# One matmul per sequence line for u: spectrum and low-rank rows stacked as 96 weight rows

## The chip, the cores and the metric

The kernel runs on one core of one Trainium2 chip. The metric is the device time of one execution in microseconds; the time before is the median of three runs. Engine names are those of the profile: PE is the matrix engine, PEld its weight loads, DVE, ACT and POOL the vector, scalar and general engines, SP the engine that here only issues DMAs.

## The reference

`x` has the shape (8, 3136, 256): eight batches, 3136 places in a sequence, 256 channels.

```
X = rfft(x, axis=1); Y = X * (filt_r + 1j * filt_i); y = irfft(Y, n=3136, axis=1)
h = y^T @ U @ V            # U is 3136 x 32, V is 32 x 3136
u = y + h^T
out = u + relu(u @ w_ch1) @ w_ch2      # 256 -> 1024 -> 256
```

All large products are done in float16 with float32 sums.

## The kernel before

The sequence is cut as 3136 = 64 x 49: a place is 49 q + r, with q from 0 to 63 and a "line" r from 0 to 48. A batch goes through these steps.

- **f1** (`f1_units`, L432): a 64-point transform over q for each line; the result goes through ACT or DVE into `asb` and by DMA to the DRAM tensor `c1`.
- **a** (`load_a`, L451): `c1` is read back in the other order, eight frequencies to a tile, 98 rows (49 lines, real and imaginary).
- **middle** (`stream`): per step m, `px` = forward transform over the lines (L466), the products with the filter on DVE (L485, L487; their sum on POOL, L490), `pi` = inverse transform over the lines (L502), evacuated by ACT into `esb` (L506). A step's `pi` is made two steps behind its `px` (LAG = 2). After four steps SP writes `esb` to the DRAM tensor `c2` (L508).
- **e** (`load_e`, L458): `c2` is read back into `e2`, 64 spectrum rows per line. Two lines stand one above the other, so that a tile of 128 rows holds 24 pairs of lines and the last line; one batch is one tile, and there are two such tiles. Four pairs of DMAs of 200 and 192 KB fill one.
- **h1** (`h1_unit`, L533): h1 = U^T y, from `e2` and the transformed U (`usb`), 25 matmuls into four column quarters of one PSUM tile that L537 (ACT) scales into the 128-row tile `h1` (four partial sums, not folded).
- **u** (`u_part`, in `make_u` and `make_odd`): for four pairs of lines and one half dh of the channels, one matmul of 512 columns adds the low-rank part (weights `h1`, moving `vr`, which holds V four times on top of itself, L555), and four of 128 columns add y itself (weights `e2`, moving the inverse 64-point transform `s2`, L560). ACT evacuates (L591, L594). The last line of each batch goes in `make_odd`, with 64 columns.
- **the channel network**: `mm1` (L601, evacuated with relu by L609 on ACT or L607 on DVE) and `mm2` (L627 or, "turned", L656, followed by L660 and L661 on DVE). SP and POOL send the results out (L669); from batch 2 on each group sends four DMAs on SP.

The order of the work on every engine is written out by hand. The outer loop runs over "groups" of four pairs of lines, six to a batch, of which the eight matmul pairs of `mm1` set the beat: a group has eight slots, a batch 48 (SB). `put(slot, gen)` hangs a piece of another stage into a slot, `run(slot)` issues it; an even slot runs behind the four L601 matmuls of two `mm1`, an odd one behind a quarter of `mm2` of the group before. `make_u` of the next group is issued in the third quarter, so that the first u of batch b stands about four slots ahead of slot 48 b. Within a slot, pieces are issued in the order in which they were put: the middle step first, then loads, then h1. Batch 0 has its own opening (`first_f1`, `first_a`, `first_mid`), ahead of slot 0. PSUM has four tags: `m` (four banks), `o` (two), `x` (one, for `px`) and `f` (one, which `pi` and `ph` of h1 share).

```
    steps = [9 + 1.5 * k for k in range(NP)] + [33 + 2.87 * k for k in range(NP)]
    for b in range(3, nb):
        steps += [SB * (b - 2) + 31 + 3 * k for k in range(NP)]
    ...
            put(t + (4 if b else 3), one(load_e, b + 1, m // GP))
    ...
        put(SB * b - 4, h1_unit(b))
```

V is brought into its layout in the opening: 14 POOL copies (L266), then seven matmuls with the selection matrix `sel` (L277, 32 weight rows) and seven ACT copies (L278) into `vr`, one of each in the opening and six in slots 1 to 11.

Of the kernel before, what the change touches and what calls it, by code (L numbers as in the profile page):

```python
# [21 lines left out]
KG = 8  # L22
# [4 lines left out]
def _consts():  # L27
# [21 lines left out]
    for s in range(NS):  # L49
        for j in range(49):  # L50
# [29 lines left out]
    return (w64.astype(f16), s2.astype(f16), np.eye(128).astype(f16),  # L80
            np.tile(np.eye(32), (1, 4)).astype(f16),
            np.ascontiguousarray(t2.transpose(1, 0, 2).reshape(98, NS * 128)).astype(f16),
# [5 lines left out]
def kernel(  # L88
# [12 lines left out]
    nb = x.shape[0]  # L101
    w64_np, s2_np, idn_np, sel_np, t2_np, g_np = _consts()
    w64_d = nc.inline_tensor(w64_np, name="w64d")
    s2_d = nc.inline_tensor(s2_np, name="s2d")
    idn_d = nc.inline_tensor(idn_np, name="idnd")
    sel_d = nc.inline_tensor(sel_np, name="seld")
    t2_d = nc.inline_tensor(t2_np, name="t2d")
# [35 lines left out]
    def load_x(b, c, parts=None):  # L143
        if c not in st[b].setdefault("x", {}):
            st[b]["x"][c] = sb.tile([128, 9 * DM], F16, tag="xt", bufs=6, name="xt")
        t = st[b]["x"][c]
        for lo, hi in parts or ((c0[c], c0[c + 1]),):
            for h in range(2):
                m = (hi - lo) // 4
                nc.gpsimd.dma_start(  # L150
                    t[64 * h:64 * h + 64, (lo - c0[c]) * DM:(lo - c0[c] + 4 * m) * DM]
                    .rearrange("p (m e) -> p m e", m=m),
                    bass.AP(tensor=x.tensor, offset=x.offset + (b * SEQ + 2 * lo + 4 * h) * DM,
                            ap=[[RD, NQ], [8 * DM, m], [1, 4 * DM]]))
            if hi == NH:
                o = (NH - 1 - c0[c]) * DM
                if b:
                    nc.gpsimd.memset(t[64:128, o:o + DM], 0.0)
                nc.gpsimd.dma_start(t[0:64, o:o + DM], rows(x, b, NR - 1, 1))
# [60 lines left out]
    for c in range(1, len(CH)):  # L220
        load_x(0, c)
    sel = cst.tile([32, 128], F16)
    nc.sync.dma_start(sel, sel_d.ap())
    s2 = cst.tile([128, 128], F16)
# [11 lines left out]
    load_x(1, 2)  # L236
    uq = sb.tile([64, NR * RANK], F16, tag="esb", bufs=2, name="uq")
    nc.gpsimd.dma_start(uq, moe_U.rearrange("(q r) p -> q (r p)", q=NQ))
    vqs = []
    for k in range(2):  # L240
        v = sb.tile([32, SEQ // 2], F16, tag="xt", bufs=6, name="vq")
        vqs.append(v)
        nc.gpsimd.dma_start(v, moe_V[:, k * (SEQ // 2):(k + 1) * (SEQ // 2)])
    w1 = cst.tile([128, 2 * 1024], F16)
# [7 lines left out]
    nc.gpsimd.dma_start(w2n, moe_w_ch2.rearrange("(t cc) e -> cc t e", t=8))  # L252
    vr = cst.tile([128, NH * 128], F16)
    usb = cst.tile([128, NH * RANK], F16)
    nc.vector.memset(usb[64:128, (NH - 1) * RANK:NH * RANK], 0.0)

    vps = []

    def v_order():

        for r0 in range(0, NH, 4):
            n, nh = (4, 2) if r0 < NH - 1 else (1, 1)
            vp = sb.tile([32, 512], F16, tag="h", bufs=18, name="vp")
            dst = vp[:, 0:n * nh * 64].rearrange("p (r h q) -> p r h q", h=nh, q=64)
            for k, v in enumerate(vqs):
                nc.gpsimd.tensor_copy(  # L266
                    dst[:, :, :, 32 * k:32 * k + 32],
                    bass.AP(tensor=v.tensor, offset=v.offset + 2 * r0,
                            ap=[v.ap[0], [1, n], [4, nh], [NR, 32]]))
            vps.append((r0, n * nh * 64, vp))  # L270
            yield

    def v_units():

        for r0, n, vp in vps:
            pv = bank("m", "pv")
            nc.tensor.matmul(pv[:, 0:n], sel[:, :], vp[:, 0:n], start=True, stop=True)  # L277
            nc.scalar.copy(vr[:, r0 * 128:r0 * 128 + n], pv[:, 0:n])  # L278
            yield

    def new_e2(b):
        e2 = sb.tile([128, NH * DM], F16, tag="e2", bufs=2, name="e2")
        (nc.gpsimd if b else nc.vector).memset(e2[64:128, (NH - 1) * DM:NH * DM], 0.0)
        st[b]["e2"] = e2
        return e2

    def prep_u():
        for n0, nn in ((0, 16), (16, 9)):
            pu = bank("o", "pu")
            for h in range(2):  # L290
# [3 lines left out]
                    bass.AP(tensor=uq.tensor, offset=uq.offset + (2 * n0 + 4 * h) * RANK,  # L294
                            ap=[uq.ap[0], [8 * RANK, k], [1, 4 * RANK]]),
                    start=True, stop=True, skip_group_check=True)
            if nn % 4:
                nc.tensor.matmul(pu[0:64, (nn - 1) * RANK:nn * RANK], w64[0:64, 0:64],
                                 uq[:, (NR - 1) * RANK:NR * RANK],
                                 start=True, stop=True, skip_group_check=True)  # L300
# [6 lines left out]

    at = sb.tile([128, 2 * 64 * NR], F16, tag="e2", bufs=2, name="at")
    atv = at.rearrange("p (e k r) -> p e k r", e=2, r=NR)
# [38 lines left out]
    def first_a(m):  # L348
        gi, ml = divmod(m, KG // 2)
        if ml == 0:  # L350
            st[0].setdefault("a", {})[gi] = sb.tile([98, KG * DM], F16, tag="a2", bufs=4, name="a2")
        pt = bank("o", "pt")
# [9 lines left out]
    def first_mid(fill):  # L362

        et = sb.tile([128, 2 * NH * 128], F16, tag="e2", bufs=2, name="et")
        etv = et.rearrange("p (e r h k) -> p h e r k", e=2, h=2, k=64)
# [38 lines left out]
        back(*pend)  # L404
        e2 = new_e2(0)
        for k4, n0 in enumerate(range(0, NH, 4)):
# [11 lines left out]
            if k4 in (1, 2, 3, 4):  # L418
                next(fill)
            if k4 == 5:  # L420
                next(vgen)

# [26 lines left out]
    def load_a(b, gi):  # L449
        t = sb.tile([98, KG * DM], F16, tag="a2", bufs=4, name="a2")  # L450
        nc.sync.dma_start(t.rearrange("p (k d) -> p k d", d=DM), spec(c1[b], gi))  # L451
        st[b].setdefault("a", {})[gi] = t

    def load_e(b, gi):
        if gi == 0:
            new_e2(b)
        for h, o, n in span(0, NH):
            nc.sync.dma_start(st[b]["e2"][64 * h + 16 * gi:64 * h + 16 * gi + 16, 0:n],  # L458
                              c2[b].ap()[16 * gi:16 * gi + 16, o:o + n])

# [62 lines left out]

    def one(load, b, k):
        load(b, k)
        yield

    def h1_unit(b):
        e2 = st[b]["e2"]
        ph = bank("f", "ph")  # L530
        for r in range(NH):
            j = 32 * (r % 4)
            nc.tensor.matmul(ph[j:j + 32, 0:DM], usb[:, r * RANK:(r + 1) * RANK],  # L533
                             e2[:, r * DM:(r + 1) * DM], start=(r < 4), stop=(r >= NH - 4),
                             tile_position=(0, j), skip_group_check=True)
        h1 = sb.tile([128, DM], F16, tag="h1", bufs=2, name="h1")
        nc.scalar.mul(h1, ph[:, 0:DM], 1.0 / ESC)  # L537
        st[b]["h1"] = h1
        yield
# [10 lines left out]

    def u_part(b, r0, nr, half, pm, o, dh):

        e2, h1 = st[b]["e2"], st[b]["h1"]
        k = 64 if half else 128
        nc.tensor.matmul(pm[:, o:o + nr * k], h1[:, dh * 128:(dh + 1) * 128],  # L555
                         vr[:, r0 * 128:r0 * 128 + nr * k], start=True, stop=False,
                         skip_group_check=True)
        for rr in range(nr):
            a = (r0 + rr) * DM + dh * 128
            nc.tensor.matmul(pm[:, o + rr * k:o + (rr + 1) * k], e2[:, a:a + 128],  # L560
                             s2[:, 0:k], start=False, stop=(rr == nr - 1),
                             skip_group_check=True)

# [4 lines left out]
    def make_odd(b):  # L568
# [3 lines left out]
        for dh in range(2):  # L572
            u_part(b, NH - 1, 1, True, pm, dh * 64, dh)
        a = 64 * (b % 2)
# [4 lines left out]
    def make_u(gx):  # L579
        b, r0, nr = groups[gx]  # L580
        if nr == 1:
            make_odd(b)
            uts[gx] = odd[b // 2]
            return
        uts[gx] = sb.tile([128, 1024], F16, tag="ut", bufs=3, name="ut")
        for dh in range(2):
            pm = bank("m", "pu")
            u_part(b, r0, nr, False, pm, 0, dh)
            dst = uts[gx][:, dh * 512:(dh + 1) * 512]
# [109 lines left out]
    fill = f1_units(1, True)  # L699
    vgen = v_units()  # L700
    first_mid(fill)
    next(h1_unit(0))
    make_u(0)

    steps = [9 + 1.5 * k for k in range(NP)] + [33 + 2.87 * k for k in range(NP)]
    for b in range(3, nb):
        steps += [SB * (b - 2) + 31 + 3 * k for k in range(NP)]
    steps += [steps[-1] + 3 * (k + 1) for k in range(LAG)]
    mid = stream()
    for k, t in enumerate(steps):  # L710
        put(t, mid)
        b, m = divmod(k - LAG, NP)
        if k >= LAG and m % GP == GP - 1:
            put(t + (4 if b else 3), one(load_e, b + 1, m // GP))
    for b in range(1, nb):
        for gi in range(NS // KG):
            t = steps[NP * (b - 1) + GP * gi]
            put(t - 9, one(load_a, b, gi))
        put(SB * b - 4, h1_unit(b))
        if b > 1:  # L720
# [8 lines left out]

    for k in range((NH - 1) // 4):  # L730
        put(1 + 2 * k, vgen)
# [50 lines left out]
```

## Time and profile before

| | |
|---|---|
| median of three runs | 550.72 us (550.3 to 551.09) |
| the profiled execution's own time | 552.23 us |
| its span | 550.1 us |
| granted PE clock, mean over the span | 0.981 |
| PE / DVE / ACT / POOL busy | 511.7 / 398.1 / 373.5 / 285.4 us |
| matmuls | 3611 |
| DMA moved | 89.76 MB, 113318 packets |

The span runs from the first to the last instruction; the 2.1 us between the span and the execution's own time lie around it. Busy shares are means over stages; the opening of batch 0 takes the first 61 us and is bound by the loads, the rest is one long run of PE work. A matmul's duration (379 ns for 512 columns) is from its start to its modelled end; how much PE time it takes is seen from the distance of the starts.

### The profile page before, as it was taken

How to read it: one execution, taken by the hardware profiler on the slowest of the kernel's cores; microseconds unless marked ns; L12 is line 12 of the kernel's file. 1: busy time of each engine (PE TensorE's matmuls, PEld its weight loads, DVE VectorE, ACT ScalarE, POOL GpSimd, SP SyncE). 2: the span in 40 equal slices, each digit the busy share in tenths (PEclk: the TensorE clock that was granted, in tenths of full speed). 3: DMA queues.
4: the chain of work that ended last, by engine and by line, in shares of the span. 5: the costliest groups of instructions: out<-in, count | busy, mean ns of one | idle time of the engine just before them, and what ended most of it. 6: DMA issues, size and time to landing. Idle time of an engine off the chain costs nothing.

```text
span 550.1 us, 10345 instructions
## 1 busy us (share of the span) xinstructions
PE 511.7 (93%) x3611; PEld 308.1 (56%) x3611; DVE 398.1 (72%) x575; ACT 373.5 (68%) x757; POOL 285.4 (52%) x408
## 2 busy tenths in 40 slices
PE   3766999998999999999999999999999999989995
PEld 3654567775676775545555555555555554544444
DVE  6874357675777667887888878887888788636563
ACT  2656676675776768777877788787776576654541
POOL 7666531253555645567767775776565555522000
PEclk9878899999999999999999999999999999999998
DMA  8999997995878867887899888998876564743444
GB/s 127 179 185 209 176 194 180 193 192 131 214 166 197 195 175 163 201 171 184 197 192 199 186 191 165 200 182 205 169 189 135 130 140 95 136 80 67 76 71 93
DMA packets 113318, 89.76 MB, mean 163 GB/s; under 512 B 51665, under 2 KB 98802, under 8 KB 112370
## 3 DMA queue, kind: packets, MB, share of 16 engines
q0 software_dynamic: 21984, 42.52, 39.2%
q1 hardware_dynamic: 91122, 46.26, 38.8%
q8 instruction: 28, 0.46, 0.4%
q10 hardware_dynamic: 160, 0.33, 0.2%
q14 instruction: 24, 0.20, 0.1%
HBM read 56.80 MB, written 48.17 MB: 191 GB/s over the span
## 4 chain that ended last, share of the span: by engine, by line
PE 75%; DVE 9%; DMA 6%; ACT 4%; issue 3%; POOL 2%; SPq 0%; ACTq 0%; DVEq 0%; POOLq 0%
PE phh L601 25%; PE po L656 19%; PE po L627 9%; PE px L466 5%; PE pi L502 4%; DMA xt<-in_x_dram 4%; DVE uv L487 4%; PE pu L555 3%; PE pu L560 3%; PE pf L432 3%; ACT h L609 2%; DVE uv L485 1%; DMA c<-asb 1%; PE ph L533 1%; DVE uv L474 1%
## 5 line engine op out<-in xcount | busy, mean ns | idle before, releaser
L609 ACT ACTIVATE h<-phh 128x512 f16<-128x512 f32 (+1 forms) x376 | 198.6, 577 | 86.6 <-PE phh L601 86.4
L601 PE MATMUL phh<-ut,w 128*128 128x512 f16 x768 | 197.3, 379 | 1.1 <-DVE h L607 0.6
L490 POOL TENSOR_TENSOR y<-uv 128x512 f16<-128x512 f16 x96 | 110.9, 1157 | 107.6 <-DVE uv L487 76.5
L656 PE MATMUL po<-h,w 128*128 128x512 f16 x560 | 143.7, 379 | 0.0
L487 DVE TENSOR_TENSOR uv<-px,ft 64x512 f16<-64x512 f32 x192 | 132.1, 688 | 2.6
L601 PEld LDWEIGHTS <-w 128*128 128x128 f16 x832 | 78.3, 98 | 76.3 <-issue 3.0
L669 POOL DMA_DIRECT2D out_dram<-och x120 | 69.8, 590 | 44.0 <-DVE och L661 37.9
L485 DVE TENSOR_TENSOR uv<-px,ft 128x512 f16<-128x512 f32 x96 | 64.8, 675 | 36.9 <-PE px L466 36.2
L506 ACT CAST esb<-pi 98x512 f16<-98x512 f32 x112 | 66.2, 591 | 34.1 <-PE pi L502 29.1
L656 PEld LDWEIGHTS <-w 128*128 128x128 f16 x560 | 52.9, 98 | 49.7
L660 DVE TENSOR_TENSOR tt<-po,ut 128x512 f32<-128x512 f32 x70 | 48.4, 692 | 40.0 <-PE po L656 24.1
L438 ACT CAST asb<-pf 128x512 f16<-128x512 f32 (+1 forms) x83 | 47.9, 577 | 19.9 <-PE pf L432 19.0
L627 PE MATMUL po<-w,h 128*128 128x256 f16 x448 | 58.0, 273 | 0.0
L466 PE MATMUL px<-a,t 98*128 98x256 f16 x256 | 50.2, 278 | 5.5 <-DVE uv L487 2.6
L661 DVE STREAM_TRANSPOSE och<-tt 128x512 f32<-128x512 f32 x70 | 49.8, 711 | 2.4
L474 DVE TENSOR_TENSOR uv<-px,ft 128x1024 f16<-128x1024 f32 x32 | 38.4, 1221 | 14.6 <-PE px L466 14.2
L627 PEld LDWEIGHTS <-h 128*128 128x128 f16 x448 | 42.9, 98 | 9.4
L466 PEld LDWEIGHTS <-t 98*128 98x128 f16 x256 | 22.9, 100 | 32.5 <-DVE uv L487 10.9
L432 PE MATMUL pf<-xt,w 128*128 128x512 f16 (+1 forms) x91 | 35.0, 387 | 6.4 <-DMA xt<-in_x_dram 5.7
L555 PE MATMUL pu<-vr,h 128*128 128x512 f16 (+1 forms) x112 | 38.5, 353 | 1.7 <-ACT h L537 1.5
L591 ACT CAST ut<-pu 128x512 f16<-128x512 f32 x70 | 38.1, 607 | 1.8 <-PE pu L560 1.6
L560 PEld LDWEIGHTS <-e 128*128 128x128 f16 x400 | 30.7, 98 | 15.4 <-issue 0.6
(83 smaller groups left out, 479.8 us busy)
## 6 DMA issues: line engine op xcount, KB each, us to landing
xt<-in_x_dram POOLq DMA_DIRECT2D x46, 256.0 KB, 6.9
a<-c SPq DMA_DIRECT2D x28, 392.0 KB
c<-esb SPq DMA_DIRECT2D x28, 392.0 KB
out_dram<-och SPq DMA_DIRECT2D x160, 64.0 KB, 2.8
c<-asb POOLq DMA_DIRECT2D x30, 256.0 KB, 4.2
out_dram<-och POOLq DMA_DIRECT2D x120, 64.0 KB, 3.4
out_dram<-och POOLq DMA_DIRECT2D x24, 256.0 KB, 4.4
e<-c SPq DMA_DIRECT2D x28, 200.0 KB, 4.3
```

What stands on the lines that cost most here:

```text
L432: nc.tensor.matmul(pf[:, 0:w], w64[:, :], xt[:, n0 * DM:n0 * DM + w], start=True, stop=True)
L466: nc.tensor.matmul(px[:, sl * DM:(sl + 1) * DM], t2[:, s * 128:(s + 1) * 128], a2[:, (2 * ml + sl) * DM:(2 * ml + sl + 1) * DM], start=Tru ...
L485: nc.vector.tensor_mul(uv[:, 0:512], px[:, :], ft[:, a:a + 512])
L487: nc.vector.tensor_mul(uv[p:p + 64, 512:1024], px[q:q + 64, :], ft[q:q + 64, b:b + 512])
L490: nc.gpsimd.tensor_add(y, uv[:, 0:512], uv[:, 512:1024])
L506: nc.scalar.copy(split(esb[:, ml * 512:(ml + 1) * 512]), natural(pi[0:98, :]))
L555: nc.tensor.matmul(pm[:, o:o + nr * k], h1[:, dh * 128:(dh + 1) * 128], vr[:, r0 * 128:r0 * 128 + nr * k], start=True, stop=False, skip_gr ...
L601: nc.tensor.matmul(pm[:, 0:w], w1[:, dh * 1024 + t * 128:dh * 1024 + (t + 1) * 128], ut[:, dh * w:(dh + 1) * w], start=(dh == 0), stop=(dh ...
L609: nc.scalar.activation(h[:, 0:w], pm[:, 0:w], RELU)
L627: nc.tensor.matmul(po[:, o:o + DM], hs[gx, t][:, rr * 128:(rr + 1) * 128], w2[:, t * DM:(t + 1) * DM], start=(t == 0), stop=False, skip_gr ...
L656: nc.tensor.matmul(po[:, :], w2[:, t * DM + dh * 128:t * DM + (dh + 1) * 128], hs[gx, t][:, :], start=(t == 0), stop=(t == 7))
L669: (nc.gpsimd if k and b < nb - 1 else nc.sync).dma_start(dst, och[32 * i:32 * i + 32, k * 512:(k + 1) * 512] .rearrange("p (r e) -> p r e" ...
```

## The change

From batch 1 on, the 32 rows of h1 are folded (four partial sums added by a matmul with `fold`) and placed under the 64 spectrum rows of each line, so that a line has 96 weight rows; under the 64 rows of the inverse transform lie the 32 rows of V for that line (`low`, 96 x 49*64). One matmul of 64 columns per line and channel half then gives u, and the 512-column products with V are gone. Batch 0 keeps the old layout of `e2` and adds the low-rank part from a folded h1 (`hz[0]`, with 64 rows of zeros on top) with one 512-column matmul behind the four of 128.

What goes with it: `e2` of a batch becomes two tiles of 96 rows (12 pairs of lines, and 12 pairs with the last line), three tiles in rotation in place of two of 128 rows; the DMAs of `load_e` are cut differently (three for both tiles in place of two), and for batches from 2 on the first loads of the second tile wait for slot 48 (b-1) + 13. h1 is made of 49 matmuls of 64 rows in place of 25 of 128, from `ul` (U transformed by four matmuls in slots 1 to 7). h1 is issued in three slots, 8, 7 and 6 ahead of slot 48 b, in place of one, 4 ahead: the 49 matmuls and the scaling; the fold and an ACT copy; a DVE copy of h1 beside the first four pairs of lines and four DMAs from SBUF to SBUF for the others. The middle steps are put three slots earlier (28 in place of 31, and for batches 1 and 2 at 9 + 1.4 k and 31 + 2.85 k). `xt` has five buffers in place of six, `a2` three in place of four. The seven `sel` matmuls and their ACT copies are gone, and a table of 64 x 3136 (401 KB) is loaded by SP in the opening.

```diff
-    vr = cst.tile([128, NH * 128], F16)
-    usb = cst.tile([128, NH * RANK], F16)
+    low = cst.tile([96, NR * 64], F16)
+    nc.sync.dma_start(low[0:64, :], low_d.ap())
+    ul = cst.tile([64, NR * RANK], F16)
+    hz = [cst.tile([96, DM], F16, tag=f"hz{k}", name="hz") for k in range(2)]
...
-    def v_units():
-        for r0, n, vp in vps:
-            pv = bank("m", "pv")
-            nc.tensor.matmul(pv[:, 0:n], sel[:, :], vp[:, 0:n], start=True, stop=True)
-            nc.scalar.copy(vr[:, r0 * 128:r0 * 128 + n], pv[:, 0:n])
+    def u_units():
+        for a in range(0, NR * RANK, 512):
+            n = min(512, NR * RANK - a)
+            pv = bank("m", "pv")
+            nc.tensor.matmul(pv[:, 0:n], w64[:, :], uq[:, a:a + n], start=True, stop=True)
+            nc.scalar.copy(ul[:, a:a + n], pv[0:64, 0:n])
...
+    def load_e(b, gi, ks=(0, 1)):
+        for k in ks:
+            e2 = new_e2(b, k)
+            p = slice(16 * gi, 16 * gi + 16)
+            nc.sync.dma_start(
+                e2[p, 0:24 * DM].rearrange("p (h e) -> p h e", h=2),
+                bass.AP(tensor=c2[b], offset=16 * gi * RD + 12 * k * DM,
+                        ap=[[RD, 16], [NH * DM, 2], [1, 12 * DM]]))
+            if k:
+                nc.sync.dma_start(e2[p, 24 * DM:NH * DM], c2[b].ap()[p, 24 * DM:NH * DM])
...
     def h1_unit(b):
         ph = bank("f", "ph")
+        n = NR if b else NH
+        for r in range(n):
...
+                lhs, rhs = ul[:, a * RANK:(a + 1) * RANK], e2[k][0:64, c]
...
         nc.scalar.mul(h1, ph[:, 0:DM], 1.0 / ESC)
+        yield
+        pn = bank("m", "pn")
+        nc.tensor.matmul(pn[:, 0:DM], fold[:, :], h1[:, :], start=True, stop=True)
+        row = hz[b % 2][64:96, :]
+        nc.scalar.copy(row, pn[64:96, 0:DM])
+        if b:
+            yield
+            nc.vector.tensor_copy(quad[:, :, 0:4], ...)     # row, eight times
+            for h in range(2):
+                nc.sync.dma_start(flat[:, h, 1:3], ...)     # 131 KB each
+            nc.sync.dma_start(e2[1][64:96, 0:24 * DM]..., ...)
+            nc.sync.dma_start(e2[1][64:96, 24 * DM:NH * DM], src[:, 0:DM])
         yield
...
-    def u_part(b, r0, nr, half, pm, o, dh):
-        nc.tensor.matmul(pm[:, o:o + nr * k], h1[:, dh * 128:(dh + 1) * 128],
-                         vr[:, r0 * 128:r0 * 128 + nr * k], start=True, stop=False, ...)
-        for rr in range(nr):
-            nc.tensor.matmul(pm[:, o + rr * k:o + (rr + 1) * k], e2[:, a:a + 128],
-                             s2[:, 0:k], start=False, stop=(rr == nr - 1), ...)
+    def u_part(b, r0, nr, pm, o, dh):
+        for rr in range(nr):
+            for h in range(2 if nr > 1 else 1):
+                k, a = place(r0 + rr, h)
+                r = 8 * (r0 // 4) + 4 * h + rr
+                c = o + rr * 128 + h * 64
+                nc.tensor.matmul(pm[:, c:c + 64], e2[k][:, a * DM + dh * 128:a * DM + dh * 128 + 128],
+                                 low[:, r * 64:(r + 1) * 64], start=True, stop=True, ...)
...
-    steps = [9 + 1.5 * k for k in range(NP)] + [33 + 2.87 * k for k in range(NP)]
+    steps = [9 + 1.4 * k for k in range(NP)] + [31 + 2.85 * k for k in range(NP)]
     for b in range(3, nb):
-        steps += [SB * (b - 2) + 31 + 3 * k for k in range(NP)]
+        steps += [SB * (b - 2) + 28 + 3 * k for k in range(NP)]
...
-        put(SB * b - 4, h1_unit(b))
+        gen = h1_unit(b)
+        for t in (8, 7, 6):
+            put(SB * b - t, gen)
```

## The prediction

> **What bounds the kernel.** I read the busy shares first, then the windows by stage, then the timeline of PE around the changed steps, last that of SP and ACT there.
>
> ```profile
> PE 511.7 (93%) x3611; PEld 308.1 (56%) x3611; DVE 398.1 (72%) x575; ACT 373.5 (68%) x757; POOL 285.4 (52%) x408
> ...
> 250.00:310.00 60.00, 59.10 (x378) 31.45 (x380) 49.74 (x75) 47.53 (x94) 41.35 (x58) 1.00 0.91 191
> 310.00:370.00 60.00, 59.47 (x380) 32.39 (x368) 48.95 (x73) 47.40 (x99) 40.95 (x57) 1.00 0.89 188
> ```
>
> The window rows give length, then busy time of PE, PEld, DVE, ACT, POOL, the clock and the DMA share. Over a batch of 60 us PE is busy for 59, DVE for 49: PE bounds every batch, so PE time taken away counts in full, and so does each new wait of PE. What u costs is seen from the starts:
>
> ```profile
> 300.02 0.38 PE L555 MATMUL pu<-vr,h 128*128 128x512 f16 x1
> 300.23 0.39 PE L560 MATMUL pu<-s,e 128*128 128x128 f16 x4
> 300.46 0.38 PE L555 MATMUL pu<-vr,h 128*128 128x512 f16 x1
> ...
> 127.80 0.20 PE L555 MATMUL pu<-vr,h 128*128 128x64 f16 x1
> 127.84 0.19 PE L560 MATMUL pu<-s,e 128*128 128x64 f16 x1
> 127.86 0.19 PE L555 MATMUL pu<-vr,h 128*128 128x64 f16 x1
> 127.89 0.19 PE L560 MATMUL pu<-s,e 128*128 128x64 f16 x1
> ```
>
> One channel half takes 440 ns: 215 for the 512 columns, 4 x 56 for the rest. Matmuls of 64 columns with new weights each start 29 ns apart.
>
> **PE work, batches 1 to 7.** u has 12 halves per batch, 84 in all; eight matmuls of 64 columns take 8 x 29 = 235 ns, so 84 x 0.205 = **-17.2 us**; the seven odd lines lose two of four such matmuls, 0.065 each, -0.5. h1: the 25 matmuls start at 126.94 and L555 at 127.80; without the 0.2 us of the changeover this is 28 ns each (four column quarters side by side), so 24 more cost 0.67 us per batch, +4.7. The fold has 256 columns, 109 ns by the spacing of L627: +0.8 in seven batches. The first u of an odd batch now waits for L537 (at 128.34 instead of 127.92, 0.4 us, four times); its h1 will be two slots old by then: -1.6. Together **-13.8 us**. The fold waits for nothing: a quarter of `mm2` (0.86 us) lies between, the scaling takes 0.39. The DVE copy has 2048 elements per row, as L208's row (0.69 us), and about 3 us of PE work lie between fold and first u of an odd batch (6 of an even one), against 0.75 for the ACT copy and 0.7 for its own; I take 0 (at three times the time, as if the broadcast were slow, up to 0.5 us in four batches). The four SBUF DMAs (671 KB) have about eight slots, 9 us, until group 1 needs them, and e's 192 KB land in 5: 0, too.
>
> **h1's new place.** It stands at slot 40 of the batch before instead of 44, its last `pi` at slot 31 instead of 34. Three consequences, each a wait of PE.
>
> First, slot 40 has a middle step, and its `pi` comes directly ahead of h1 in the same PSUM bank (tag `f`), in six of the seven batches in the built order. Today four L601 lie between:
>
> ```profile
> 308.47 0.38 PE L502 MATMUL pi<-y,g 128*98 128x256 f16 x2
> 308.69 1.02 PE L601 MATMUL phh<-ut,w 128*128 128x512 f16 x4
> 309.65 0.94 PE L533 MATMUL ph<-e,usb 128*32 128x256 f16 x25
> ...
> 308.89 0.59 ACT L506 CAST esb<-pi 98x512 f16<-98x512 f32 x1 [0.33 <-PE pi L502]
> ```
>
> ACT frees the bank at 309.48, 0.9 us after the second `pi` started at 308.58; behind four L601, as it will be, mostly 1.05 us. Against the 0.2 us at which h1 could follow: 0.95 us of idle PE.
>
> Second, from the last `pi` to h1 there are nine slots instead of ten (batch 1: six instead of eight), at 1.0 to 1.2 us each, and the way between is DMA:
>
> ```profile
> 474.45 1.84 SPq L669 DMA_DIRECT2D out_dram<-och  x4
> 476.95 0.32 SPq L508 DMA_DIRECT2D c<-esb  x1
> 481.31 0.78 SPq L458 DMA_DIRECT2D e<-c  x2
> ...
> 484.40 1.03 PE L601 MATMUL phh<-ut,w 128*128 128x512 f16 x4
> 486.70 0.93 PE L533 MATMUL ph<-e,usb 128*32 128x256 f16 x25 [1.27 <-DMA out_dram<-och]
> ...
> 126.94 0.92 PE L533 MATMUL ph<-e,usb 128*32 128x256 f16 x25 [1.60 <-ACT esb L506]
> ```
>
> The loads of e wait until the write of c2 has landed (4.4 us here, 3.6 mostly) and land about 5.1 us after their issue (7.4 in batch 1): 9.0 to 9.9 us, in batch 1 11.1. Batches 7 and 1 wait today, 1.3 and 1.8 us; the ACT copy named in batch 1's row ended at 125.97, so the rest was the load.
>
> Third, slot 31 stands right behind the slot where a group's four L669 are queued on SP: they wait for DVE's transposes and take 1.8 us to issue. Today the write three slots later finds SP free; now it stands behind them, at 476.3 in batch 7, although its `pi` is ready three slots earlier. Right behind other writes I let it land in 4.3 us.
>
> So for batch 7: 476.3 + 4.4 + 0.4 + 4.8 = 485.9, less 0.3 as the first twelve matmuls need only the first tile; h1 could start at 481.5 (slot 40 at 481.6, 0.3 for the changeover, 0.4 saved on u): 4.1 to 4.4 us idle against 1.3. Batch 4: L669 end at 297.7, +4.3+0.4+5.1-0.3 = 307.2 against 305.1, 2.1 us. In the same way batch 3 has 1.2, batch 5 2.0, batch 6 2.6; batch 2 (no L669 on SP) the bank alone, 0.95; batch 1 (two slots fewer, 3 us) 4.0 against 1.8. More than today: 2.2+0.95+1.2+2.1+2.0+2.6+3.1 = **+14.2 us**; from 6 (loads hidden, bank waits alone) to 19 (each DMA a little later).
>
> **The clock.** PE's clock falls after stalls that need not be long:
>
> ```profile
> 47.80:51.20 3.40, 0.98 (x14) 1.00 1.19 185
> 51.20:58.00 6.80, 5.98 (x44) 0.50 0.85 173
> ```
>
> Columns: length, PE busy, clock, DMA. A stretch with 2.4 us idle was followed by 6.8 us at half clock. The 4 us stalls of batches 1 and 7 may do the same; 3.4 to 6.8 us at half clock cost 1.7 to 3.4 each, less what the stall covers. I take **+2** (0 to 7). The Trainium skill ("TensorE: Matmul & The Clock Gate", What's actually happening) has the clock fall after at least one idle window of about 3.4 us. The rows above show a fall with less idle than that, so the measurement decides. By the page's rule alone I would put 0 to 1 for this term.
>
> **Opening.** The table `low` (401 KB) is the next DMA of SP at about 3 us, beside the first loads of x, in a stretch where the DMA share is 0.7 to 1.1 and PE waits for `xt`. At the 185 GB/s of 10 to 20 us it is 2.2 us of DMA time, part of which fills gaps: **+1.5** (0 to 2.2). Seven `sel` matmuls go, four of 512 columns come; ACT is what the chain goes through there (0.48 us a copy), two copies fewer after slot 0: **-1.0** (-1.6 to -0.5). The first u now waits for fold and copy (+0.5), against the `sel` unit ahead of it (-0.5): 0. Buffers: the third x chunk of batch 1 waits for the first chunk of batch 0, read by 9 us, and is issued after 37: 0. The second e tile's buffer is freed at slot 13, where its load stands: 0; were it late, SP's outputs and writes would queue behind it.
>
> **Sum.** -13.8 + 14.2 + 2 + 1.5 - 1.0 = +2.9 us on the span of 550.1. The profiled run's own 552.23 would become 555.1; it lies 1.5 above the median, so the median goes from 550.72 to **553.6**.
>
> **Rivals.**
> 1. *The loads are hidden* (faster). The write isn't held by L669, because DVE runs ahead after each stall; then 7.3 in place of 14.2, clock 0.5, opening 1: -6 us, **544.7**. For it: L669 ended 0.7 to 2.4 us ahead of the write today. Against it: batch 7 waits already.
> 2. *The waits grow* (slower). Each boundary a microsecond later through the SBUF copies and the extra e DMA, and the half clock at four of them, place PE at slot 40 of each batch: 19 and 6 in place of 14.2 and 2: +12, **562**. It decides once a stall passes some 2.4 us. For it: in today's loads single e DMAs took 7 to 8 us.
> 3. *64 columns don't hold 29 ns in a row.* The trace has them only in fours. At 56 ns, as for 128 columns, the gain on u is gone: +18, **571**. Against it: 25 h1 pairs at 28 ns. The Trainium skill (same page, "Wait — 56ns, not 53.3ns?") gives about 62 ns per matmul where the sequencer decodes in ucode; the 28 ns rows disagree.
> 4. That the change doesn't do what it says is excluded: the built order has 686 matmuls of 64 columns, 49 per h1, and no `sel`.
>
> **Numbers.** Forecast 0.55 (with its own spread of some 3 us: slower 0.41, same 0.09, faster 0.05), rival 1 0.30, rival 2 0.12, rival 3 0.03. Faster 0.35, same 0.09, slower 0.56, where same means within 0.2%, 1.1 us, about what a measurement of this kernel can tell from no change. The range reaches from a little under rival 1 to just short of rival 2, 543.5 to 560.5, and leaves out rival 3, most of rival 2 and the best end of rival 1.
>
> **What would show it.** Right: PE idle of 1 us ahead of h1 in batch 2 and of over 3 us in batches 1 and 7, named to ACT or DMA; L508 right behind L669 on SP; u halves of 235 ns; clock under 1.0 near 125 or 482 us. Wrong: h1 behind `pi` with under 0.5 us idle, e loads landed ahead of slot 40, u halves over 300 ns, or a first wait of u for the DVE copy.

## The result, and the profile after

The changed kernel takes **605.57 us** (median of four runs, 598.73 to 613.37) against 550.9 for the kernel before on the same chip: a ratio of 1.087, with an interval of 1.078 to 1.096. The forecast was 553.6 with a range to 560.5: the sign was right, the size far off. The profiled execution took 598.73 us, span 597.0 (before: 552.23 and 550.1), so the trace has 46.9 us to explain. Medians here and below are over all executions, while the ratios leave out the slow ones, more than 1.5% above their kernel's fastest (here 610.33 and 613.37); the traces of new_no_sbuf_dma, new_writes_act and new_keep are of such slow executions and are read for the place of a wait more than for its size.

First the page's row of busy times, then the window rows of after (columns as before: length, busy PE, PEld, DVE, ACT, POOL, clock, DMA share, GB/s):

```profile
PE 518.8 (87%) x4022; PEld 309.5 (52%) x4022; DVE 404.3 (68%) x583; ACT 375.9 (63%) x762; POOL 285.7 (48%) x402
```

```profile
250.00:310.00 60.00, 52.30 (x367) 27.53 (x364) 43.00 (x64) 39.95 (x79) 35.06 (x48) 0.94 0.82 177
310.00:370.00 60.00, 52.59 (x387) 28.65 (x386) 42.14 (x62) 41.35 (x88) 32.95 (x46) 0.94 0.80 169
```

PE was busy for 59.1 and 59.5 of 60 us at a clock of 1.00; now it is busy for 52.3 and 52.6 at 0.94. No other engine has filled up, and the DMA share has not risen (0.91 and 0.89 before). PE waits, and after waiting it runs slower. The waits list of PE says for what (us in total, times, longest):

```profile
PE ph L560 <- DMA e<-c: 26.2, 14, 5.0
PE px L484 <- DMA a<-c: 13.2, 7, 3.5
```

Neither row exists before, beyond h1's 1.3 and 1.6 us. To make a balance I took the start of every matmul from slot 0 on: its own time is its columns at 2.4 per ns plus 2.5 ns, which gives the distances of starts seen in a row (216 ns for 512 columns, 56 for 128, 29 for 64); h1's, four side by side, count 28 ns each (where nothing holds them up, 25 start within 0.67 us and 49 within 1.32). What passes beyond this until the next start is idle, and what it costs more in stretches at half clock is counted apart.

| us from slot 0 to the last matmul | before | after | difference | forecast |
|---|---|---|---|---|
| PE work | 462.1 | 449.4 | -12.7 | -12.2 |
| idle around h1 | 4.8 | 35.6 | +30.8 | +14.2 |
| idle ahead of `px` | 7.5 | 26.1 | +18.6 | 0 |
| other idle | 6.2 | 6.5 | +0.3 | -1.6 |
| extra by the half clock | 0 | 14.1 | +14.1 | +2 |
| start of slot 0 | 62.6 | 58.3 | -4.3 | +0.5 |

The differences add up to +46.8, the forecasts to +2.9 (the prediction's -13.8 holds 1.6 us of waits of the first u, which stand under "other idle" here). The last row isn't the change's: among the experiments with the same opening, new_x_late starts slot 0 at 64.6 us.

**The u matmuls are as forecast.** First both halves of a group on PE, 16 matmuls, with what follows; then the DVE copy, which was taken to hide:

```profile
280.79 0.63 PE L603 MATMUL pu<-low,e 96*128 96x64 f16 x16
281.25 1.03 PE L732 MATMUL po<-h,w 128*128 128x512 f16 x4
```

```profile
268.00 0.68 DVE L571 COPY e<-hz 32x2048 f16<-32x2048 f16 x1 [7.89 <-ACT hz L567]
```

The two halves take 0.46 us together, 29 ns a matmul, where one half alone took 0.44 before. The broadcast copy takes 0.68 us, and the first u waits for it only 0.6 us in the whole run.

**h1 of batch 3**, on PE and on SP (start, duration, what; in brackets the idle time before and what ended it):

```profile
255.84 1.03 PE L677 MATMUL phh<-ut,w 128*128 128x512 f16 x4
257.53 0.38 PE L484 MATMUL px<-a,t 98*128 98x256 f16 x2 [0.66 <-DVE och L737]
257.74 0.38 PE L520 MATMUL pi<-y,g 128*98 128x256 f16 x2
262.13 0.83 PE L560 MATMUL ph<-e,ul 64*32 64x256 f16 x12 [4.01 <-DMA e<-c]
263.24 2.29 PE L560 MATMUL ph<-e,ul 64*32 64x256 f16 x37 [0.28 <-DMA e<-c]
```

```profile
247.73 1.83 SPq L745 DMA_DIRECT2D out_dram<-och  x4
249.66 0.40 SPq L526 DMA_DIRECT2D c<-esb  x1
250.16 0.51 SPq L465 DMA_DIRECT2D a<-c  x1
254.94 0.78 SPq L472 DMA_DIRECT2D e<-c  x2
255.76 0.41 SPq L477 DMA_DIRECT2D e<-c  x1
```

The order is the one forecast: the write of c2 stands right behind four outputs (L745), h1 right behind the `pi` with which it shares a bank. The durations aren't. The write landed at 254.9, 5.3 us after its issue (3.3 to 4.5 for the writes ahead of h1 before; 4.3 forecast); the three loads of e landed 7.1, 7.9 and 7.7 us after theirs (4.8 to 5.1 forecast), with two loads of x and two writes of c1, about 1 MB, issued between 253.6 and 256.2. The first twelve matmuls run on the first tile, then PE stops again for the second. And the clock pays once more (length, PE busy, ..., clock, DMA share, GB/s):

```profile
258.30:261.70 3.40, 0.00 (x0) 0.00 (x0) 1.78 (x3) 0.45 (x1) 3.07 (x5) 1.00 1.11 185
261.70:265.10 3.40, 2.69 (x48) 2.00 (x49) 0.00 (x0) 0.00 (x0) 0.00 (x0) 0.50 0.84 255
265.10:268.50 3.40, 3.40 (x17) 1.20 (x9) 0.50 (x1) 0.75 (x2) 0.00 (x0) 0.50 0.01 1
```

A stall of 4 us was followed by 6.8 us at half clock, most of them full of work. There are eight stretches at half clock between slot 0 and the last matmul, of 3.4 or 6.8 us, 44.4 us in all; before there is none.

**The wait the forecast left out** is that of `px` for `a`. On POOL, SP and PE:

```profile
226.26 2.35 POOL L745 DMA_DIRECT2D out_dram<-och  x4 [0.44 <-DVE och L737]
228.61 1.11 POOL L456 DMA_DIRECT2D c<-asb  x2
```

```profile
234.86 0.32 SPq L465 DMA_DIRECT2D a<-c  x1
```

```profile
240.63 0.38 PE L484 MATMUL px<-a,t 98*128 98x256 f16 x2 [2.37 <-DMA a<-c]
```

The last write of c1 stands behind four outputs on POOL and is issued at 228.6 and 229.2; it lands at 234.8; only then can the load of `a` start; it lands at 240.5, and `px` had been due since 238. In the waits of SP's queue, "L465 <- DMA c<-asb" is 26.4 us in 8 times, where L451 of before has 5.9 in 4. The middle steps, the f1 pieces and the loads of x move together by three slots, the outputs of a group do not, so this chain met other neighbours.

### The profile page after: what moved, and what is told of

It is laid out like the page before. It is cut to its first block, busy times and chain, and to the rows that moved or that the text cites. A ratio compares the mean times of both kernels' runs of the same rounds, so it can differ in the third digit from the quotient of the medians.

```text
span 597.0 us, 11269 instructions
## 1 busy us (share of the span) xinstructions
PE 518.8 (87%) x4022; PEld 309.5 (52%) x4022; DVE 404.3 (68%) x583; ACT 375.9 (63%) x762; POOL 285.7 (48%) x402
## 5 line engine op out<-in xcount | busy, mean ns | idle before, releaser
L677 PE MATMUL phh<-ut,w 128*128 128x512 f16 x768 | 201.5, 384 | 2.1 <-DVE h L683 0.9
L732 PE MATMUL po<-h,w 128*128 128x512 f16 x560 | 148.9, 389 | 0.0
L505 DVE TENSOR_TENSOR uv<-px,ft 64x512 f16<-64x512 f32 x192 | 132.2, 688 | 2.6
L745 POOL DMA_DIRECT2D out_dram<-och x120 | 69.8, 589 | 54.5 <-DVE och L737 47.8
L732 PEld LDWEIGHTS <-w 128*128 128x128 f16 x560 | 52.3, 99 | 54.5 <-issue 5.9
L484 PE MATMUL px<-a,t 98*128 98x256 f16 x256 | 49.5, 275 | 21.4 <-DMA a<-c 13.2
L703 PE MATMUL po<-w,h 128*128 128x256 f16 x448 | 60.2, 279 | 0.0
L560 PE MATMUL ph<-e,ul 64*32 64x256 f16 x343 | 19.5, 373 | 27.0 <-DMA e<-c 26.2
L520 PE MATMUL pi<-y,g 128*98 128x256 f16 x192 | 36.7, 272 | 0.1
```

Source lines behind the costliest of these rows:

```text
L484: nc.tensor.matmul(px[:, sl * DM:(sl + 1) * DM], t2[:, s * 128:(s + 1) * 128], a2[:, (2 * ml + sl) * DM:(2 * ml + sl + 1) * DM], start=Tru ...
L505: nc.vector.tensor_mul(uv[p:p + 64, 512:1024], px[q:q + 64, :], ft[q:q + 64, b:b + 512])
L677: nc.tensor.matmul(pm[:, 0:w], w1[:, dh * 1024 + t * 128:dh * 1024 + (t + 1) * 128], ut[:, dh * w:(dh + 1) * w], start=(dh == 0), stop=(dh ...
L703: nc.tensor.matmul(po[:, o:o + DM], hs[gx, t][:, rr * 128:(rr + 1) * 128], w2[:, t * DM:(t + 1) * DM], start=(t == 0), stop=False, skip_gr ...
L732: nc.tensor.matmul(po[:, :], w2[:, t * DM + dh * 128:t * DM + (dh + 1) * 128], hs[gx, t][:, :], start=(t == 0), stop=(t == 7))
L745: (nc.gpsimd if k and b < nb - 1 else nc.sync).dma_start(dst, och[32 * i:32 * i + 32, k * 512:(k + 1) * 512] .rearrange("p (r e) -> p r e" ...
```

## The experiments

S is the theory that the place of the middle steps and of h1 in the slots costs the time; T that it is the new traffic (three e DMAs, SBUF copies). Medians are shown with the ratio to the kernel before on the same chip.

**old_u_new_slots**: the kernel before, with nothing changed but the slots.

```diff
-    steps = [9 + 1.5 * k ...] + [33 + 2.87 * k ...]
+    steps = [9 + 1.4 * k ...] + [31 + 2.85 * k ...]
-        steps += [SB * (b - 2) + 31 + 3 * k for k in range(NP)]
+        steps += [SB * (b - 2) + 28 + 3 * k for k in range(NP)]
-        put(SB * b - 4, h1_unit(b))
+        put(SB * b - 8, h1_unit(b))
```

> The old u, h1 and loads of e, with the changed kernel's slots alone: middle steps at 9 + 1.4 k, 31 + 2.85 k and 28 + 3 k, h1 eight slots ahead of its batch. Theory S (slots: the last writes of c1 and c2 of a batch now stand right behind the output DMAs, and h1 is one slot nearer to them): the waits come with the slots. Of the changed kernel's 46.9 us, about 50 are waits for loads at h1 and at the forward transform and 14.7 the half clock behind them, and only the cut of PE work (14.7) and the earlier opening (4.2) belong to the new u; so this kernel has no gain to set against the waits: 585 to 610 us. Theory T (traffic: the 671 KB from SBUF to SBUF per batch and the loads of e cut in three make every landing later): none of that is here, so 551 to 560 us, the bank wait of about 1 us at six boundaries included.

599.3 us, ratio 1.086 (1.081 to 1.091). PE's waits:

```profile
PE ph L533 <- DMA e<-c: 15.7, 4, 4.8
PE ph L533 <- DMA out_dram<-och: 9.9, 2, 5.4
PE px L466 <- DMA a<-c: 8.7, 6, 3.6
```

The slots alone, with the old matmuls, DMAs and traffic, lose some 48 us, with the same waits (56.2 us idle, 11.8 by the clock; in the second row, which names an output, h1 starts as e lands). S holds, and T isn't needed for these 48 us. But the changed kernel isn't faster than this run, although it has 12.7 us less PE work: it has 12.0 us more idle time and 2.3 more by the clock. So part of its waits comes with the new form in these slots; whether by its longer way to u or by its traffic isn't shown.

**new_no_sbuf_dma**: the changed kernel with the four SBUF DMAs replaced by two more DVE copies from `hz` (32 x 4096 and 32 x 6400), in slots 2 ahead of and 3 behind slot 48 b.

> The changed kernel with the four SBUF-to-SBUF DMAs of each batch replaced by two DVE copies of 4096 and 6400 elements per row (about 1.4 and 2.1 us of DVE per batch), in slots 2 ahead of and 3 behind the start of the batch. Theory S: the waits at h1 and at the forward transform stay, 590 to 605 us against 598.7. Theory T: without the 4.7 MB the landings are as before, waits at h1 fall from 31 us above those of before to under 10, 560 to 575 us.

640.9 us, ratio 1.162. Both theories missed it. The groups of DVE by shape (busy, mean ns of one):

```profile
L579 DVE COPY e<-hz 32x6400 f16<-32x6400 f16 x7 | 24.3, 3477 | 0.2
L575 DVE COPY e<-hz 32x4096 f16<-32x4096 f16 x7 | 8.5, 1218 | 0.2
```

The larger copy took 3.48 us, 0.54 ns per column against 0.30 for the smaller. DVE has the products behind it, so `px` waits for its bank (18.6 us named to L505, 4.3 in the changed kernel). It shows that DVE has no room for this, not that the SBUF DMAs are free; but they aren't needed for the loss either, as the experiment before lacks them and is as slow.

**new_steps_26**: the middle steps earlier still (9 + 1.3 k, 29 + 2.85 k, 26 + 3 k), h1 left where it is.

> The changed kernel with the middle steps two slots earlier (9 + 1.3 k, 29 + 2.85 k, 26 + 3 k): the last write of c2 is ready at slot 29, ahead of the outputs of slot 30, the last write of c1 at slot 13, ahead of those of slot 14, and between the last inverse transform and h1 there are eleven slots; h1 no longer follows a middle step in its slot. Theory S: the waits at h1 fall to a few us in all and with them the half clock; the cut of PE work shows: 535 to 550 us. Theory T: landings stay as late as they are (e 7 to 8 us after issue), two slots gain some 2.5 us at each of seven boundaries and a little of the clock: 565 to 580 us.

567.05 us, ratio 1.027 (1.021 to 1.033). Two slots recover some 33 us by the ratios, less than S expected: h1's waits for e fall from 26.2 to 8.3 us, but `px` still waits 12.3 us for `a`. The time lies in T's range, but not for T's reason: from batch 4 on the last loads of e land 4.7 to 6.2 us after their issue, not 7 to 8.

**new_writes_act**: the writes of c1 and c2 issued by ACT, so that they pass the outputs on SP and POOL.

```diff
-                nc.sync.dma_start(spec(c2[b], gi), ...)
+                nc.scalar.dma_start(spec(c2[b], gi), ...)
...
-                        (nc.sync if b == 1 else nc.gpsimd).dma_start(c1[b]..., ...)
+                        (nc.sync if b == 1 else nc.scalar).dma_start(c1[b]..., ...)
```

> The changed kernel with its slots, but with the writes of c2 (and of c1 from batch 2 on) issued by ACT behind its own evacuation instead of by SP (POOL) behind the output DMAs. Theory S: the write leaves about 2.4 us earlier at each boundary and lands in 3.6 us or a little more instead of 5.2, so e lands some 3 to 4 us earlier; h1 waits for 1 to 3 us instead of 3 to 6, the first forward step of a batch no longer waits, the clock falls less often: 555 to 575 us. ACT pays some 0.4 us for each of about 70 issues, off the path. Theory T: the queue a write stands in does not matter much, the landings do: 590 to 600 us.

603.1 us, ratio 1.086: no gain, against what S expected. `px` waits less for `a` (8.9 us), but two single waits of h1 reach 7 us. SP's waits say why:

```profile
SPq L472 <- DMA c<-asb: 16.1, 4, 5.5
```

In batch 3 the write of c2 landed 3.5 us after its issue, in place of 5.3. But the loads of e behind it (L472) then stood on SP for 5.1 us, until a write of c1 had landed, which they don't read but whose semaphore they wait for; in batches 4 and 5 it was the same. So the run moved a wait and doesn't test whether the place of the write costs the time.

**new_u_old_slots**: the new u with the old middle slots and h1 at 6, 5 and 4 slots ahead.

> The new u with the middle steps where they were before the change (9 + 1.5 k, 33 + 2.87 k, 31 + 3 k) and h1 in slots 6, 5 and 4 ahead of its batch, two later than in the changed kernel and the latest that still stands ahead of the first u. Theory S (the slots made the loss, the new u is a gain): the forward step no longer waits (18.6 us back), h1 waits about 1 to 2 us at a boundary since e lands about five slots ahead of the batch, the first u of four batches waits about 1 us for the DVE copy, the clock stays up but for one or two falls; the cut of 14.7 us and the earlier opening are set against some 12 us: 540 to 555 us. Theory T (extra DMA traffic of the new layout): the e loads land later here too, 7 us after issue, h1 waits 3 us and more with half clock behind: 565 to 585 us.

581.0 us, ratio 1.058 (1.053 to 1.063). PE's waits:

```profile
PE ph L560 <- DMA e<-c: 12.4, 10, 4.3
PE pu L603 <- DVE e L571: 9.0, 4, 2.8
```

S had expected 540 to 555. The time lies in T's range of 565 to 585, but e landed 3.9 to 5.2 us after its issue in batches 2 and 4 to 7, not the 7 us that T named. With the old slots the waits for `a` are down to 1.2 us, but the new chain (loads of e, h1, scaling, fold, copy on ACT, copy on DVE, u) is longer and has no slack there: now u itself waits for the copy (0.6 us in the changed kernel).

**old_u_steps_only**: the kernel before with the new middle slots, h1 left at 4.

> The kernel before with the middle steps at the changed kernel's slots and h1 left four slots ahead of its batch. It takes the h1 half of the slots' loss away and leaves the other: the last write of c1 behind the outputs of slot 14 on POOL, that of c2 behind those of slot 30 on SP. If the two are separate, h1 waits go to about 1 to 3 us a boundary and the forward step still waits some 10 to 19 us in all, with part of the half clock: 565 to 580 us. If the forward step's waits come only from the h1 stall (the order of the DMAs behind it), they vanish with it: 550 to 556 us.

561.1 us, ratio 1.020 (1.014 to 1.026), between the two expectations. `px` waits 6.8 us for `a`, in five times, and the idle time ahead of `px` is 18.4 us in place of 7.5; h1 waits no more than before. So by the ratios moving the steps alone costs 11 us, nearly all of it at `px`, and moving h1 in addition the other 36.

**new_keep**: 48 matmuls of 128 columns that nobody reads, ahead of each h1, so that PE is busy while it would wait.

> The changed kernel with 48 matmuls of 128 columns whose result nobody reads (2.7 us at full clock) ahead of the 49 of h1 at each of seven boundaries. They stand where PE waits for e anyway, 3 to 6 us in five batches and 1 to 2 us in two. If the half clock behind the stalls is a cost of its own (14.7 us of the changed kernel), it goes down by a half or more and the time falls to 585 to 593 us, although PE has 19 us more work. If the clock is only a sign of the stall, the time is the changed kernel's or up to 5 us above: 598 to 606 us.

596.6 us, ratio 1.084 (1.074 to 1.093). With 19 us more PE work it isn't slower than the changed kernel; h1's waits for e fall to 9.9 us, the time at half clock from 44.4 to 30.7 us. The clock still falls at the waits of `px`. The time lies between the two expectations, and its interval overlaps that of the changed kernel (1.078 to 1.096). That PE was idle in these places anyway is shown; what the half clock costs on its own isn't.

**new_x_late**: the loads of x six slots later (62 in place of 68).

> The changed kernel with the loads of x from batch 3 on six slots later, so that the one of slot 34 no longer runs beside the last loads of e. In the changed kernel those land 7 to 8 us after their issue (5 before the change). If the collision with x makes that, they land in about 5 us, h1 waits 2 us less at five boundaries, with less half clock: 580 to 590 us. If the collision is with the writes of c1 and the outputs, nothing much moves: 595 to 603 us.

590.1 us, ratio 1.072 (1.063 to 1.081). The waits for e fall from 26.2 to 17.0 us, those for `a` from 13.2 to 8.8. In batches 3 to 5 the loads of e land 4.8 to 5.8 us after their issue, in place of 6.5 to 8.0. So 8 us by the ratios, 14 by the waits, come from the crowding of the loads of e and a with those of x; the clock's part stays (13.9 us).

**new_steps_23**: the middle steps five slots earlier than in the changed kernel (9 + 1.25 k, 28 + 2.7 k, 23 + 3 k), with the first loads of e held until slot 48 b - 3, where their tile is free.

> The changed kernel with the middle steps a whole group (eight slots) earlier than before the change: 9 + 1.25 k, 28 + 2.7 k, 23 + 3 k; the first load of e of a batch waits for its buffer's slot. The writes then stand to the output DMAs as they did before the change, and from the last inverse transform to h1 (slot 40) there are fourteen slots, about 16 us, against a DMA chain of 11 to 15 us. Theory S' (the new u adds fold, copies and a second tile to the way from e to u; it needs h1 four slots earlier, and the loss is only that the schedule has no slack for that): waits at h1 under 1 us each, first u without a wait, forward waits as before (about 6 to 8 us), clock up throughout; the cut of 14.7 us and the earlier opening show: 530 to 545 us. If the new layout's traffic makes the landings late whatever the slots: 555 us and more.

556.2 us, ratio 1.010 (1.007 to 1.014): no gain, where 530 to 545 was expected, though not for late loads: from batch 2 on e lands 2.4 to 5.6 us ahead of h1, and no h1 waits for it. Batch 1, whose steps are pressed to 1.25 slots, still does:

```profile
130.11 0.83 PE L560 MATMUL ph<-e,ul 64*32 64x256 f16 x12 [3.26 <-DMA e<-c]
```

**old_u_steps_23**: the kernel before with these slots, h1 at 4.

> The kernel before with those same middle steps, h1 left four slots ahead: the control for what the slots alone bring to the old u. Theory S': it had only small waits for e (3 us in all), so 0 to 4 us faster than before, 545 to 551 us; the difference to the new u at the same slots is then the new u's own worth, 8 to 16 us.

560.2 us, ratio 1.016 (1.012 to 1.020): 9 us slower than before, where 0 to 4 us faster was expected. With the same middle slots the new form is 3 to 4 us faster, not the 8 to 16 expected.

**old_u_h1_6**: the kernel before with only h1 two slots earlier.

> The kernel before with h1 alone moved, from four to six slots ahead of its batch, as in the new u with old slots (574.9 us in its profile). e landed 0.6 to 2.4 us ahead of h1 before the change, and two slots are 2.2 us: h1 waits some 0.5 to 2 us at each of seven boundaries more, 1 or 2 falls of the clock: 555 to 562 us. What the new u with old slots loses beyond that (12 us and more, with its PE cut of 14 us on top) belongs to the longer way through fold and DVE copy and to the loads in three pieces. If instead this kernel is at 570 us or more, the place of h1 alone explains it.

560.8 us, ratio 1.015 (1.008 to 1.022), as expected: 8 us or so for two slots, 10.2 us of waits at L533 for DMAs. With the old middle slots e isn't there six slots ahead.

**new_u_from_2**: new_steps_23 with the new form from batch 2 on only. Batch 1 keeps the 128 spectrum rows, with h1 at slot 43, and the middle steps spread again.

```diff
-    steps = [9 + 1.25 * k ...] + [28 + 2.7 * k ...]
+    steps = [9 + 1.5 * k ...] + [30 + 2.85 * k ...]
-        for t in (8, 7, 6):
+        for t in (5, 4) if b == 1 else (8, 7, 6):
...
-            if b:
+            if b > 1:
                 u_part(b, r0, nr, pm, 0, dh)
```

> The changed u from batch 2 on; batch 1 keeps the old form (128 spectrum rows with 128 columns, h1 beside them as one matmul of 512 columns per half, no broadcast), its h1 at slot 43, and its middle steps spread as in the kernel before (9 + 1.5k); batch 2's steps 30 + 2.85k, later ones as in new_steps_23. Theory S (the time is lost where the earlier slots press the chain of px, pi, write, load, h1, and batch 1 is the place that new_steps_23 left): the 4.3 us of idle PE at batch 1's h1 and about half of the 8 us of idle PE between 69 and 110 us go, the old form costs 12 x 0.2 - 0.7 = 1.7 us: new_steps_23's 556.2 less 6 gives 549 to 552, level with the kernel before. Rival C (the rest is not batch 1's, but spread over all batches, a few tenths at each px and pi beside busier ACT, DVE and queues): no gain, 555 to 558.

**549.9 us** (12 runs) against 550.9 (17 runs): ratio 0.9999, interval 0.9965 to 1.0033. The 6 us expected of batch 1 are there, and the kernel is level with the one before. Its windows, and the h1 of batches 1 and 3 with the pieces beside them:

```profile
243.00:303.00 60.00, 58.16 (x428) 31.37 (x427) 50.27 (x75) 48.30 (x95) 41.41 (x57) 1.00 0.94 203
303.00:363.00 60.00, 58.60 (x443) 32.16 (x442) 49.91 (x74) 47.67 (x100) 41.09 (x57) 1.00 0.90 200
```

```profile
126.96 0.28 PE L717 MATMUL po<-idn,ut 128*128 128x128 f16 x2
127.16 0.94 PE L569 MATMUL ph<-e,usb 128*32 128x256 f16 x25
...
250.62 1.03 PE L687 MATMUL phh<-ut,w 128*128 128x512 f16 x4
251.58 1.59 PE L569 MATMUL ph<-e,ul 64*32 64x256 f16 x49
253.10 0.39 PE L449 MATMUL pf<-xt,w 128*128 128x512 f16 x1
```

The clock is back at 1.00, and h1 of batch 1 (the second row) and of batch 3 wait for nothing. But in the balance PE's work is 451.3 us, 10.8 less than before, and idle time 26.1, 7.6 more. What is left is small waits of the middle steps, for their one PSUM bank and for POOL's sums:

```profile
PE px L493 <- DVE uv L514: 6.9, 15, 1.0
PE pi L529 <- POOL y L517: 2.2, 3, 1.2
```

(2.6 and 1.1 us before.) Whether the new form makes these or the place of the steps was tried with the last two.

**new_u_from_2_at22** and **new_u_from_2_at25**: the same with the steps of batches 3 to 7 one slot earlier and two slots later (22 and 25 in place of 23).

> new_u_from_2 with the middle steps of batches 3 to 7 one slot earlier (start 22 instead of 23). Theory P (the remaining half-microsecond waits of px for its one bank and of pi for y depend on which slots of a group the steps meet): the waits of px and pi move by 3 to 6 us, 544 to 547 or 553 to 556. Rival F (they come with the new form, whatever the phase; the loads of e have 2 us to spare at start 23): 549 to 551.

> new_u_from_2 with the middle steps of batches 3 to 7 two slots later (start 25 instead of 23). Theory P: as for start 22, a shift of 3 to 6 us either way. Rival F: e's loads, which land 2 to 3.7 us ahead of h1 at start 23, are now about level with it, some 0 to 1 us of wait in five batches: 550 to 556, with the waits at h1 and not at px.

563.3 us, ratio 1.021 (1.017 to 1.026), and 559.2 us, ratio 1.013 (1.010 to 1.016). The place decides, and by more than expected; for start 22 the earlier place is the worse one. Its SP and PE (first a load of `a` and the `px` that waits for it, then h1 of batch 3):

```profile
210.49 0.31 SPq L535 DMA_DIRECT2D c<-esb  x1
210.86 0.87 SPq L468 DMA_DIRECT2D a<-c  x1
```

```profile
220.01 0.38 PE L493 MATMUL px<-a,t 98*128 98x256 f16 x2 [2.15 <-DMA a<-c]
...
257.71 0.38 PE L529 MATMUL pi<-y,g 128*98 128x256 f16 x2
258.93 1.58 PE L569 MATMUL ph<-e,ul 64*32 64x256 f16 x49 [0.84 <-ACT esb L533]
```

The load of `a` lands 9.0 us after its issue; with start 23 its counterpart, issued 1.4 us behind the last output on POOL in place of 0.2, takes 6.6 and is in time. The waits for `a` are 8.8 us again, against 0.7. And with 28, 25 and 22, which differ by threes, a middle step falls into slot 40 with h1, so that h1 waits 0.8 us for the bank that `pi` holds; with 23 it doesn't. (With start 25, this wait is 4.3 us in five times, and e is level with h1: 1.0 us.)

## Why the prediction was wrong

What failed is the account of the waits: the term for h1's new place was half of what it measured, the start of the middle steps had no term, and the clock, which follows both, was counted at two stalls.

- **PE work** was right: -12.2 forecast, -12.7 measured, with 235 ns per u half (230 measured) and +0.67 us for the 49 matmuls of h1 (1.52 us to the next start in place of 0.87). The 1.6 us of waits of the first u that were to go aren't seen (other idle time +0.3). The copies beside u were rightly hidden, and rival 3 is out.
- **"In h1's new place" the bank wait** was right where it shows alone: 0.95 us forecast (1.05 less 0.2, its own figures, is 0.85), 1.0 of idle time at h1 of batch 3 with start 22. In the changed kernel longer waits cover it.
- **The way from `pi` to h1 was mis-sized**: +14.2 us forecast, +30.8 measured. The order on SP was read rightly, and the write stood behind L669's counterpart as forecast; but the transfers were priced with the landings of the old schedule. The forecast's way, 4.3 + 0.4 + 5.1 - 0.3, is 9.5 us; in batch 3 it took 12.5 from the write's issue to the first matmul (1.2 us of idle PE forecast there, 4.3 measured). The loads of e now went out beside those of x and the writes of c1. The new_x_late run shows that for x: h1's waits for e fall by 9 us when x moves away; for the writes of c1 it isn't tested. Each DMA moved should have been set against what is issued in its new place.
- **A step was missing**: the middle steps also start at `px`, whose input `a` waits for the last write of c1. The forecast followed only the end of the middle stage (`pi` to h1), not its start; its sum has nothing for the 18.6 us. In old_u_steps_only this alone is 11 us.
- **The clock**: +2 forecast, +14.1 measured. The prediction saw rightly that a partly idle stretch is enough, but went by the length of a stall and counted two; eight were followed by half clock. The Trainium skill's page "TensorE: Matmul & The Clock Gate" (What's actually happening) has the fall behind at least one idle window of about 3.4 us; that fits batch 3 above, where the first row has no PE work at all. The stall of `px` at 238 us shows that less is enough, as the rows of the kernel before had:

```profile
237.80:241.20 3.40, 1.03 (x12) 0.57 (x10) 1.54 (x4) 1.21 (x3) 1.70 (x3) 1.00 1.19 294
241.20:244.60 3.40, 3.40 (x24) 1.59 (x21) 1.99 (x3) 1.56 (x3) 2.36 (x3) 0.51 0.67 96
```

  But length alone doesn't decide. The longest stall of `px`, 3.5 us up to 171.2, was followed by none:

```profile
166.20:169.60 3.40, 1.50 (x10) 0.62 (x8) 2.68 (x5) 1.34 (x3) 1.15 (x1) 1.00 1.02 225
169.60:173.00 3.40, 1.82 (x29) 1.73 (x30) 1.32 (x2) 1.18 (x3) 0.00 (x0) 1.00 0.58 188
```

  In this trace the eight falls begin whole multiples of 3.41 us apart (121.8, 190.1, 241.3, 261.7, 330.0, 401.7, 466.5 and 528.0 us). In the 3.41 us ahead of each, PE was busy for at most 1.2 us; the stall at 171 lay across two such steps and left 1.5 and 1.8 us of work in them. In the traces of all runs, from slot 0 to the last matmul, each such step at full clock with less than 1.4 us of PE work was followed by half clock, none with more than 2.4 us was, and between the two both occur.

- **Rival 2, "the waits grow"**, had the direction, with a chance of 0.12 and a price of 562. It put the later landings down to the SBUF copies and the extra e DMA, but old_u_new_slots lacks both and is as slow; and it took each boundary a microsecond later, where measured were two or three, at h1 and at `px`, which it didn't name.
- **Rival 1** fell as argued against it. The **opening** can't be told apart from the spread between executions.

What stays open: why the new form turns most of its shorter PE work into waits, all of it in the changed kernel's slots and 7.6 of 10.8 us in new_u_from_2. The steps are now packed in less PE time while DVE's work per batch is the same; that it is this is argued, not shown. And for a schedule that uses the shorter u, only the starts 22, 23 and 25 were tried.

## What to carry to other kernels

Where a hand-made order is moved, follow every chain that the moved piece belongs to at both ends, from its first load to its last user, and price each DMA by what will be in flight beside it in the new place, not by its landing in the old one. A cut of 13 us in the work of the bounding engine can be lost several times over by a move of three slots: run the schedule alone, with the old arithmetic, before judging the arithmetic. On an engine whose clock falls with idleness, a stall can cost more than its length: here the eight that a fall followed, some 33 us in all, cost 14 us more.

## What the runs showed of the hardware that was not expected

- A DVE copy from a broadcast row took 0.68 us for 32 x 2048 and 1.22 for 32 x 4096, but 3.48 for 32 x 6400: 0.33, 0.30 and 0.54 ns per column.
- One 392 KB load landed 6.6 us after its issue in one schedule and 9.0 in another that issued it 1.2 us nearer to the outputs ahead of it.
- With the writes of c1 and c2 issued by ACT, loads of e on SP stood for 5.1 to 5.5 us in three batches until a write of c1 landed that they don't read (new_writes_act).
- Whether half clock followed a stall depended on how the stall lay in steps of 3.41 us: in the changed kernel it did behind steps with up to 1.2 us of PE work, and didn't behind steps with 1.5 us and more.
